# Narrowing of the third and fourth dense weight placed after the last step of attention, in a fused attention, dense layer and soft mixture of experts

## The chip, the cores and the metric

The kernel runs on one core of a Trainium2 chip. The metric is the device time of one execution in microseconds (us); the time of a kernel is the median of its runs. The engines are named as the profile names them: PE is TensorE's matmul, PEld its weight load, DVE is VectorE, ACT is ScalarE, POOL is GpSimd, SP is SyncE, whose queue issues the DMAs.

## The reference, cut

Three layers follow each other. Attention has 4 batches, 8 heads, 576 positions and head size 64, with a bias that depends on the position. A dense layer with a leaky activation (512 to 2048 to 512) works on the 2304 tokens, and a soft mixture of 8 experts comes last.

```
scores = scale * q @ k.T + bias;  attn = softmax(scores);  x = attn @ v      # x: 2304 x 512
h = x @ w_in                                       # 512 -> 2048
g = np.maximum(h, 0.0) + alpha * np.minimum(h, 0.0)
y = g @ w_out                                      # 2048 -> 512
logits = y @ phi                                   # soft mixture of experts follows
```

The dense weights are handed over as 64-bit floats, and the kernel narrows them to 32 bits itself.

## The kernel before

**Attention.** 16 pairs (four head pairs times four batches) have 9 tiles of 128 rows each, 144 tiles in all. `Attention.run` walks them two at a time in 72 steps. For one tile PE forms the scores `s` (L379), DVE adds the bias and takes the row's extreme in one custom instruction (`z`, `m`, L397), ACT takes the exponential `e` (L416), PE transposes it (`t`, L433), ACT and DVE copy the transposed halves out of PSUM (`g`, L457), and PE multiplies with `v` (`o`, L472). The scores of a tile are formed four tiles ahead. Every one of these instructions is held in the order of the program (`keep_in_program_order`), from the second pair on. PE's `o` products come in two halves per pair, 256 and 320 columns wide, each in a piece of twelve and a piece of eight records.

**The dense layer.** The 2304 tokens are six blocks (0 to 5) of 384, the 2048 hidden columns are 16 pieces `f`. For each block and piece, `up` forms `h` from `x` and the weight (L695, twelve matmuls in three terms of high and low parts), ACT takes two relus (L703, L705), DVE joins them into `g` (L706), ACT rounds `g` to its high part `gr` (L714), DVE or POOL forms the low part (L716), and `down` adds into `ys` (L728, nine matmuls). Blocks 0 and 1 run interleaved, block 1 two pieces behind.

**A dense weight's way in.** `w_load(f)` (L647, on SP's queue) brings 1 MB of 64-bit weights into one of two slots of the tile `stage`. `w_narrow(f)` makes 32-bit floats `wr` out of them with three DVE instructions (L641, L643, L644; 128 x 1024 each), and then issues `w_load(f + 2)` into the slot that it has read. `w_split` then makes the high part on ACT (L677: `w2h`, `w3h`, ...) and the low part on DVE in one piece (L679) or on POOL in four (L684). The tile `stage` lies in the space of an attention bias tile (`take_stage`, two steps before step 54), which is free when the third head pair no longer needs it. The first two weights (f = 0, 1) go another way, through the tile `early`, in twelve half pieces during attention (`half_piece`). For f = 2 and 3, `w_load` is called in step 52; their `w_narrow` is called by `prep` in `Moe.run`, behind attention, and isn't held in the order of the program. A scheduler that models the engines' times orders what isn't held; it may pull such an instruction forward in the order of its engine.

**Steps.** `extra` is a table of calls per step: `at(step, f, ...)` adds one, and `run` makes them at the step's end. Steps 46, 49, 52, 55, 64 and 69 also rescale and split columns of `x` for the dense layer (L604, L1176, L1181).

Of the kernel before, what the change touches and what calls it, by code (L numbers as in the profile page):

```python
# [67 lines left out]
NEARLY = 2  # L68
# [493 lines left out]
class Moe:  # L562
# [88 lines left out]
        pool, tag = self.homes[f] if f < len(self.homes) else (self.wring, "raw")  # L651
        return pool.tile([P, 1024], dtype, tag=tag, name=name)

    def w_narrow(self, f):

        self.raw[f] = self.raw_tile(f, f"wr{f}")
        for k in range(3):
            self.narrow(self.raw[f], self.slots[f % 2], k)
        if f + 2 < NF:
            self.w_load(f + 2)  # L660

# [464 lines left out]
def kernel(  # L1126
# [11 lines left out]
    att = Attention(tc, ident, W, xT, rs, qk, v_l)  # L1138
# [11 lines left out]
    moe = Moe(tc, ident, xT, rs, w_l, None, x0, x1)  # L1150
# [40 lines left out]
    def at(step, f, *args):  # L1191
        extra.setdefault(step, []).append(lambda: f(*args))
# [7 lines left out]
        at(step + 1, x_low, blk, c, c % 2)  # L1200
    for k in range(6 * NEARLY):
        at(HSTEPS[k], moe.half_piece, k // 3, k % 3)
    at(STAGE - 2, take_stage)
    for f in range(2):
        at(STAGE - 2, moe.w_load, NEARLY + f)
# [142 lines left out]
```

## Time and profile before

| what | value |
|---|---|
| median of 3 runs | 843.49 us |
| lowest and highest | 841.05 and 844.2 us |
| the profiled execution | 850.17 us |
| its span in the trace | 848.4 us |
| PE busy in the span | 779.9 us (92%) |
| DVE busy in the span | 550.8 us (65%) |

All stretches are given in the span's own time, counted from its start. Attention's scores start at 85.8 us, its last product ends at 341 us; the dense layer follows, and the first product of the experts starts at 791.6 us. A busy share is an average over these stages. What a moved instruction is worth is read in the stretch that it leaves and in the one that it enters.

### The profile page before, as it was taken

To read this page: it belongs to the slowest core of one execution; us is meant where nothing else is said; L and a number is where in the kernel's file an instruction comes from. 1 tells how busy PE (TensorE), PEld (TensorE's weight loads), DVE (VectorE), ACT (ScalarE), POOL (GpSimd) and SP (SyncE) were. 2 spreads that over 40 slices of the span, in tenths; PEclk is the share of its full clock that TensorE was granted. 3 is DMA by queue.
4 is the path that set the end of the run, shared out by engine and by line. 5 is a ranking of instruction groups with operands and counts; after the bars stand their busy time and mean duration, and the time that the engine had idled before them with its cause. 6 is when DMAs were issued, how large, how long until landed. Compare 5 with 4: busy or idle time off the path is not lost.

```text
span 848.4 us, 18810 instructions
## 1 busy us (share of the span) xinstructions
PE 779.9 (92%) x7444; PEld 641.5 (76%) x7444; DVE 550.8 (65%) x1058; ACT 489.6 (58%) x1066; POOL 334.6 (39%) x423
## 2 busy tenths in 40 slices
PE   6875698999998999999999999999999999998993
PEld 6875576777765777898899888888888889987341
DVE  8765477888989986899434746575656546555102
ACT  8832466787777686443445665656556556655002
POOL 6974243555464330414323352435345233242000
PEclk9989598999999899999999999999999999999897
DMA  6799994863947421365100200050010005338985
GB/s 205 180 215 199 217 215 149 215 197 117 250 121 252 146 77 48 123 221 203 45 0 1 66 10 1 2 188 10 1 29 1 1 5 187 107 110 292 412 353 224
DMA packets 59784, 114.46 MB, mean 135 GB/s; under 512 B 10672, under 2 KB 38192, under 8 KB 57904
## 3 DMA queue, kind: packets, MB, share of 16 engines
q1 hardware_dynamic: 59696, 113.26, 43.9%
q8 instruction: 58, 0.95, 0.5%
q14 instruction: 30, 0.25, 0.1%
HBM read 91.95 MB, written 21.29 MB: 133 GB/s over the span
## 4 chain that ended last, share of the span: by engine, by line
PE 62%; DMA 17%; DVE 13%; ACT 3%; issue 3%; SPq 1%; POOL 0%; DVEq 0%; ACTq 0%; POOLq 0%
PE ys L728 17%; PE h L695 17%; PE o L472 9%; PE s L379 6%; PE t L433 6%; DMA ep<-in_mw_dram 4%; PE acc L165 3%; DMA rb<-rs 3%; DMA W<-rows 3%; DMA stage<-in_w_dram 2%; DMA xT<-xo 2%; DVE wr L643 2%; DVE mask L149 2%; DVE wr L644 2%; DMA em<-in_mw_dram 1%
## 5 line engine op out<-in xcount | busy, mean ns | idle before, releaser
L706 DVE SCALAR_TENSOR_TENSOR g<-g,nal 128x384 f32<-128x384 f32 x96 | 73.2, 763 | 83.6 <-ACT g L705 83.4
L416 ACT ACTIVATE e<-z,m 128x576 f32<-128x576 f32 x144 | 110.4, 767 | 3.5 <-DVE m L397 3.2
L397 DVE CUSTOM_DVE_ANT_0 z<-s,nb 128x576 f32<-128x576 f32 x144 | 103.4, 749 | 11.5 <-PE s L379 5.6
L714 ACT ACTIVATE gr<-g 128x384 fp32r<-128x384 f32 x95 | 49.8, 524 | 98.8 <-DVE g L706 98.8
L433 PEld LDWEIGHTS t<-ident,e 64*128 64x128 f32 x1440 | 68.7, 144 | 49.0 <-ACT g L457 12.2
L457 ACT ACTIVATE g<-t 128x320 f32<-128x320 f32 x144 | 62.2, 432 | 60.6 <-PE t L433 47.4
L433 PE MATMUL t<-ident,e 64*128 64x64 f32 x1440 | 81.8, 234 | 16.3 <-ACT g L457 9.2
L472 PE MATMUL o<-g,v 128*64 128x256 f32 (+1 forms) x640 | 94.6, 418 | 0.0
L457 DVE COPY g<-t 128x320 f32<-128x320 f32 x144 | 69.5, 486 | 30.8 <-PE t L433 25.4
L165 PE MATMUL acc<-wp,mask 128*128 128x64 bf16 (+1 forms) x1680 | 60.3, 202 | 19.7 <-issue 8.5
L716 DVE TENSOR_TENSOR gr<-g,gr 128x384 fp32r<-128x384 f32 x79 | 52.8, 668 | 34.0 <-ACT gr L714 33.9
L165 PEld LDWEIGHTS <-mask 128*128 128x128 bf16 (+1 forms) x1680 | 58.0, 106 | 21.9 <-issue 12.5
L703 ACT ACTIVATE g<-h 128x384 f32<-128x384 f32 x96 | 46.6, 485 | 43.3 <-PE h L695 41.2
L379 PE MATMUL s<-kh,qh 64*128 64x288 f32 x320 | 61.0, 352 | 10.0 <-DVE rows L190 5.8
L345 POOL TENSOR_SCALAR qh<-raw 128x608 fp32r<-128x608 f32 x32 | 21.8, 698 | 114.2 <-PE s L379 109.8
L716 POOL TENSOR_TENSOR gr<-g,gr 128x384 fp32r<-128x384 f32 x16 | 20.9, 1308 | 109.6 <-ACT gr L714 106.1
L472 PEld LDWEIGHTS o<-g,v 128*64 128x64 f32 x640 | 41.2, 137 | 24.7 <-issue 0.7
L146 ACT ACTIVATE mask<-pr,wb 128x576 bf16<-128x576 f16 (+4 forms) x81 | 46.9, 669 | 22.4 <-PE acc L165 22.4
L379 PE MATMUL s<-kh,ql 64*128 64x288 f32 x320 | 53.9, 309 | 0.0
L379 PE MATMUL s<-kl,qh 64*128 64x288 f32 x320 | 53.9, 309 | 0.0
L348 POOL TENSOR_TENSOR ql<-raw,qh 128x304 fp32r<-128x304 f32 x64 | 53.1, 862 | 0.0
L705 ACT ACTIVATE g<-h 128x384 f32<-128x384 f32 x96 | 46.5, 485 | 0.0
(1008 smaller groups left out, 2058.4 us busy)
## 6 DMA issues: line engine op xcount, KB each, us to landing
ep<-in_mw_dram SPq DMA_DIRECT2D x30, 512.0 KB
raw<-in_qk_dram SPq DMA_DIRECT2D x16, 896.0 KB
stage<-in_w_dram SPq DMA_DIRECT2D x14, 1024.0 KB
nb<-W SPq DMA_DIRECT2D x12, 576.0 KB
v<-in_v_l_dram SPq DMA_DIRECT2D x16, 320.0 KB
pre<-in_mw_dram SPq DMA_DIRECT2D x10, 512.0 KB
ex<-in_mw_dram SPq DMA_DIRECT2D x9, 512.0 KB
em<-in_mw_dram SPq DMA_DIRECT2D x8, 512.0 KB
```

Source lines behind the costliest of these rows:

```text
L165: nc.tensor.matmul(dst[:, u // 8, :, :, 4 * (u % 8) : 4 * (u % 8) + 4], mask[:, (16 * k + u) % RING, cols], wp[:, part], start=part == 0, ...
L348: self.nc.gpsimd.tensor_tensor(st[x, 1][:, c], src[:, c], st[x, 0][:, c].bitcast(F32), ALU.subtract)
L379: nc.tensor.matmul(s[:, hf, :288], st["q", a][d, o : o + P], st["k", b][d, 288 * h : 288 * h + 288], start=n_ == 0, stop=n_ == len(seq) - 1,),
L397: nc.vector.tensor_tensor_reduce(out=z.rearrange("p (a b) -> p a b", a=2), in0=s[:, :, :288], in1=self.nb[st["hp"]][:, self.SLOT[t]].rearr ...
L416: self.pin(i, nc.scalar.activation(e, z, AF.Exp, bias=m, scale=-1.0, accum_out=acc))
L433: self.pin(i, nc.tensor.transpose(tp[r][:, c], e[q, k0 : k0 + P], self.ident[q, q]))
L457: self.pin(i, nc.vector.tensor_copy(dst, src) if r else nc.scalar.activation(dst, src, AF.Copy))
L472: nc.tensor.matmul(o[64 * h : 64 * h + 64, :n], st["v"][:, h, c], g[:, c, :n], start=c == 0, stop=c == 4),
L695: nc.tensor.matmul(h, w_[:, c * P : (c + 1) * P], x_[:, c], start=c == 0 and n_ == 0, stop=c == NC - 1 and n_ == 2,)
L706: nc.vector.scalar_tensor_tensor(g, neg, self.nal[:, f : f + 1], g, ALU.mult, ALU.add)
L716: eng.tensor_tensor(gl, g, gh.bitcast(F32), ALU.subtract)
L728: i = self.nc.tensor.matmul(self.ys[blk][t], g_[:, t * P : (t + 1) * P], w_[:, 512:], start=f == 0 and n_ == 0, stop=f == NF - 1 and n_ == 2,)
```

## The change

`w_narrow` gets a flag that holds its three DVE instructions in the order of the program, and the calls for f = 2 and f = 3 are entered in the table for step 72 (16 * 9 // 2), the last pass of attention's loop. `prep` then finds both weights there and no longer calls it. The two `w_load`s that `w_narrow` issues, for f = 4 and 5, move along. Nothing is computed otherwise.

```diff
-    def w_narrow(self, f):
+    def w_narrow(self, f, pin=False):
 
         self.raw[f] = self.raw_tile(f, f"wr{f}")
         for k in range(3):
-            self.narrow(self.raw[f], self.slots[f % 2], k)
+            i = self.narrow(self.raw[f], self.slots[f % 2], k)
+            if pin:
+                self.tc.keep_in_program_order(i)
         if f + 2 < NF:
             self.w_load(f + 2)
 ...
     for k in range(6 * NEARLY):
         at(HSTEPS[k], moe.half_piece, k // 3, k % 3)
+    for f in range(NEARLY, NEARLY + 2):
+        at(len(att.pairs) * 9 // 2, moe.w_narrow, f, True)
     at(STAGE - 2, take_stage)
```

In the order lists below, a name such as `g11_1_1` carries the pair (11), `z12_2` the pair and the tile, and a line from 661 on is two higher after the change than before.

On DVE, at the change from pair 11 to pair 12 (a row with - stands there only before):

```order
-L641 TENSOR_SCALAR wr2_7253<-stage_5923 128x1024
-L643 SCALAR_TENSOR_TENSOR wr2_7253<-stage_5923,wr2_7253 128x1024
 L457 COPY g11_1_1_5890<-t11_6_1_5909 128x5x64
 L493 RECIPROCAL r11_5941<-r11_5941 128x9
 L397 ISA z12_2_5959,m12_2_5960<-s12_2_5926,nb3_5498 128x576
 L397 ISA m12_2_5960 128x1
-L644 SCALAR_TENSOR_TENSOR wr2_7253<-stage_5923,wr2_7253 128x1024
-L641 TENSOR_SCALAR wr3_7322<-stage_5923 128x1024
 L397 ISA z12_3_5962,m12_3_5963<-s12_3_5933,nb3_5498 128x576
```

Four of the six narrowing instructions stand here before; the other two follow within the next ten rows. After the change the copies, `z` and `m` of attention follow each other.

On DVE, at the end of attention (`rt15` is the last copy of pair 15, `xo15_1` its last output), before:

```order
L457 COPY rt15_7164<-t15_8_1_7151 9x64
L706 SCALAR_TENSOR_TENSOR g32_7200<-g32_7200,nal_2237 128x384 x2
L480 COPY xo15_1_7184<-o15_1_7173 128x320
L641 TENSOR_SCALAR wr4_7388<-stage_5923 128x1024
L641 TENSOR_SCALAR wr5_7451<-stage_5923 128x1024
L643 SCALAR_TENSOR_TENSOR wr4_7388<-stage_5923,wr4_7388 128x1024
L643 SCALAR_TENSOR_TENSOR wr5_7451<-stage_5923,wr5_7451 128x1024
L679 TENSOR_TENSOR w3l_7328<-wr3_7322,w3h_7327 128x1024
```

and after:

```order
L643 SCALAR_TENSOR_TENSOR wr2_7173<-stage_5923,wr2_7173 128x1024
L708 SCALAR_TENSOR_TENSOR g32_7210<-g32_7210,nal_2237 128x384
L644 SCALAR_TENSOR_TENSOR wr2_7173<-stage_5923,wr2_7173 128x1024
L641 TENSOR_SCALAR wr3_7178<-stage_5923 128x1024
L643 SCALAR_TENSOR_TENSOR wr3_7178<-stage_5923,wr3_7178 128x1024
L708 SCALAR_TENSOR_TENSOR g32_7210<-g32_7210,nal_2237 128x384
L644 SCALAR_TENSOR_TENSOR wr3_7178<-stage_5923,wr3_7178 128x1024
L480 COPY xo15_1_7194<-o15_1_7183 128x320
L718 TENSOR_TENSOR gr_7211<-g32_7210,gr_7211 128x384
L641 TENSOR_SCALAR wr4_7388<-stage_5923 128x1024
L681 TENSOR_TENSOR w3l_7328<-wr3_7178,w3h_7327 128x1024
```

The narrowing of weights 2 and 3 now stands ahead of the last output copy and of the narrowing of weight 4, whose load is issued when weight 2 is done.

On PE, behind attention's last product (`h2` is block 1 with weight 0, `h3` block 0 with weight 2, `h4` block 1 with weight 1), before:

```order
L695 MATMUL h2_7295<-x1_5575,w0l_6338 128x384
L728 MATMUL ys0_0_7283<-w0h_6337,gr_7201 128x512
L728 MATMUL ys0_0_7283<-w0l_6338,gr_7201 128x512
...
L728 MATMUL ys0_2_7285<-w0h_6337,gr_7201 128x512
L695 MATMUL h3_7331<-x0_2240,w2h_7258 128x384 x2
L695 MATMUL h3_7331<-x0_2240,w2l_7259 128x384
```

and after:

```order
L697 MATMUL h2_7300<-x1_5575,w0l_6338 128x384
L697 MATMUL h3_7331<-x0_2240,w2h_7263 128x384 x2
L697 MATMUL h4_7361<-x1_5575,w1h_6544 128x384 x2
L697 MATMUL h4_7361<-x1_5575,w1l_6545 128x384
...
L697 MATMUL h4_7361<-x1_5575,w1h_6544 128x384
L697 MATMUL h3_7331<-x0_2240,w2l_7264 128x384
```

PE comes to weight 2 right behind `h2` now; before, the nine products into `ys0` stood between. The products into `ys0` with weights 0 and 1 come after `h3` and `h4` now.

## Rows read from the trace of the kernel before

**Rows 1.** The page's part 1: busy us (share of the span) and instructions.

```profile
PE 779.9 (92%) x7444; PEld 641.5 (76%) x7444; DVE 550.8 (65%) x1058; ACT 489.6 (58%) x1066; POOL 334.6 (39%) x423
```

**Rows 2.** DVE in order of time, 270 to 282 us: start, us, instruction, [idle before].

```profile
270.26 0.87 DVE L641 TENSOR_SCALAR wr<-stage 128x1024 uint32<-128x1024 uint32 x1 [1.09 <-DMA stage<-in_w_dram]
271.17 1.23 DVE L643 SCALAR_TENSOR_TENSOR wr<-stage,wr 128x1024 uint32<-128x1024 uint32 x1
...
273.45 1.22 DVE L644 SCALAR_TENSOR_TENSOR wr<-stage,wr 128x1024 uint32<-128x1024 uint32 x1
274.59 0.69 DVE L641 TENSOR_SCALAR wr<-stage 128x1024 uint32<-128x1024 uint32 x1
...
277.26 1.20 DVE L643 SCALAR_TENSOR_TENSOR wr<-stage,wr 128x1024 uint32<-128x1024 uint32 x1
...
280.15 1.20 DVE L644 SCALAR_TENSOR_TENSOR wr<-stage,wr 128x1024 uint32<-128x1024 uint32 x1
```

**Rows 3.** Waits of PE, 266 to 290 us: us in total, times, longest.

```profile
PE s L379 <- DVE m L397: 2.2, 3, 1.8
PE t L433 <- DVE g L457: 2.0, 1, 2.0
PE t L433 <- ACT g L457: 0.7, 2, 0.3
```

**Rows 4.** Busy time by stretch: stretch, us, PE, PEld, DVE, ACT, POOL, granted clock, DMA.

```profile
272.00:276.00 4.00, 1.24 (x18) 0.83 (x18) 4.00 (x10) 1.29 (x4) 0.00 (x0) 0.99 0.94 334
276.00:280.00 4.00, 3.41 (x32) 3.00 (x34) 4.00 (x10) 2.31 (x6) 0.00 (x0) 0.50 0.75 274
280.00:284.00 4.00, 4.00 (x38) 2.92 (x34) 3.98 (x9) 1.26 (x4) 0.00 (x0) 0.66 0.40 123
266.68:289.30 22.62, 17.77 (x214) 13.32 (x210) 20.25 (x43) 13.07 (x37) 8.06 (x11) 0.85 0.71 259
301.70:316.90 15.20, 14.39 (x210) 10.91 (x210) 12.74 (x36) 12.34 (x35) 3.52 (x5) 1.00 0.24 75
360.00:380.00 20.00, 20.00 (x103) 18.11 (x102) 19.29 (x23) 7.28 (x15) 2.75 (x2) 1.00 0.61 214
```

**Rows 5.** DVE in order of time, from attention's last copy on.

```profile
338.35 0.20 DVE L457 COPY rt<-t 9x64 f32<-9x64 f32 x1
342.03 1.28 DVE L641 TENSOR_SCALAR wr<-stage 128x1024 uint32<-128x1024 uint32 x2
343.23 3.44 DVE L643 SCALAR_TENSOR_TENSOR wr<-stage,wr 128x1024 uint32<-128x1024 uint32 x2
355.05 0.85 DVE L641 TENSOR_SCALAR wr<-stage 128x1024 uint32<-128x1024 uint32 x1 [1.41 <-DMA stage<-in_w_dram]
...
402.80 1.75 DVE L644 SCALAR_TENSOR_TENSOR wr<-stage,wr 128x1024 uint32<-128x1024 uint32 x1
```

**Rows 6.** ACT, POOL and the issue of weight 6's load, in order of time.

```profile
340.12 0.47 ACT L705 ACTIVATE g<-h 128x384 f32<-128x384 f32 x1
341.49 1.06 ACT L677 ACTIVATE w2h<-wr 128x1024 fp32r<-128x1024 f32 x1 [0.90 <-PE o L472]
342.63 6.33 POOL L684 TENSOR_TENSOR w2l<-wr,w2h 128x256 fp32r<-128x256 f32 x4 [1.34 <-ACT w2h L677]
350.06 43.82 SPq L647 DMA_DIRECT2D stage<-in_w_dram  x10
```

**Rows 7.** PE in order of time, from attention's last product on.

```profile
341.38 0.62 PE L695 MATMUL h<-x,w0h 128*128 128x384 f32 x2
343.58 0.40 PE L728 MATMUL ys<-w0h,gr 128*128 128x512 f32 x1
354.01 0.51 PE L695 MATMUL h<-x,w3h 128*128 128x384 f32 x2
363.07 0.51 PE L695 MATMUL h<-x,w4h 128*128 128x384 f32 x2
423.08 0.51 PE L695 MATMUL h<-x,w11h 128*128 128x384 f32 x2
```

## The prediction

> **What bounds the kernel now.** The page's part 1 comes first: PE is busy for 779.9 of 848.4 us [rows 1], so a gain has to be time in which PE waits or runs slowly. In the stretch that the change empties, around the change from pair 11 to pair 12, PE isn't the bound. DVE's rows in order of time show six narrowing instructions between attention's copies [rows 2]: the first waited 1.09 us for its DMA, which it does at the head of DVE's queue, so that the copies and `z` behind it stood too. The list of PE's waits shows who paid: PE lost 2.2 us to `m` and 2.0 us to copies on DVE, and 0.7 us to ACT, which is fed by the same chain [rows 3]. Then read the table of stretches [rows 4]: in 272 to 276 us DVE is busy for all of the 4.00 us and PE for 1.24; PE's granted clock is still 0.99 there, and in the next two stretches 0.50 (the lower level, 1.2 GHz) and 0.66. Behind the end of attention it is otherwise: in 360 to 380 us PE is busy for 20.00 of 20.00 us at full clock, with DVE at 19.29 right behind it [rows 4].
>
> **What is taken out of attention.** I measure the loss between equal points, PE's first piece of a 256-wide product. The stretch with the narrowing is 22.62 us long, the one two pairs later, with as many tiles, 15.20; PE has 214 and 210 records in them, DVE 43 and 36, and six of the 43 are the narrowing [rows 4]. The difference is 22.62 - 15.20 = 7.4 us. Two other sums agree. On PE, the waits are 2.2 + 2.0 + 0.7 = 4.9 us [rows 3]; the clock costs 4.0 x (1 - 0.50) + 4.0 x (1 - 0.66) = 3.4 us [rows 4]; of the 8.3, the later stretch has 15.20 - 14.39 = 0.8 us without PE too [rows 4], which leaves 7.5. On DVE, the six take 0.87 + 1.23 + 1.22 + 0.69 + 1.20 + 1.20 = 6.4 us, and with the wait of 1.09 that is 7.5 [rows 2]. Without them DVE has 20.25 - 6.4 = 13.9 us of work in some 15.2, so it fits, closely. **I take -7.4**; the bounds are -4.1 (only the waits go, 4.9 - 0.8, and the clock falls all the same) and -8.3 (nothing of the later stretch's idle time comes back here). The loads of weights 4 and 5 go out of this stretch as well; nobody here waits for them, and the DMA share of 0.94 and 0.75 in it [rows 4] can only fall.
>
> **What is put into the end of attention.** The loads of weights 2 and 3 have long landed there, so no wait for them goes along. DVE is free at 338.35 + 0.20 = 338.55 us [rows 5]. Its new order is L641 (0.7), the join of `h0` (0.6), L643 (1.2), the join of `h1` (0.6; ACT's relu ends at 340.6 [rows 6], in time), L644 (1.2): weight 2 is narrow at 342.8. The bound is the two L643 that ran beside POOL and took 3.44 / 2 = 1.72 each [rows 5] instead of 1.2; POOL makes low parts here too, so 343.8 is the other end. ACT's high part takes 1.06 [rows 6]: ready at 343.9, or 344.9. PE is done with `h2` when it was before, at 343.58 [rows 7], and now asks for weight 2 at once: it waits 0.3 to 1.3 us. Two matmuls later it asks for `h4`, whose PSUM buffer was `h2`'s; ACT's two relus on `h2` (0.47 each [rows 6]) stand behind the high part, which costs PE another 0.5. **So PE waits 0.8 to 1.8 us, and I take 0.8**, since the isolated durations of [rows 2] are nearer to what stands there than the four long POOL pieces beside which 1.72 was measured.
>
> Behind that I find no wait. POOL's first piece of `w2l` takes 6.33 / 4 = 1.58 [rows 6] and is there at 345.5 (346.5), while PE has the rest of `h4` before it. Weight 3 is narrow 0.7 + 1.2 + 0.6 + 1.2 = 3.7 us (with long instructions 4.8) after weight 2, at 346.5 to 348.6. Its low part stands behind the first instruction of weight 4, and so behind a DMA: that load is issued when weight 2 is done, and weight 6's took from 350.06 [rows 6] to 355.05 [rows 5], 5.0 us. So DVE waits to 347.8 (348.8), takes 0.85 [rows 5] and makes `w3l` in 1.2 to 1.7: ready by 351.4. PE came to weight 3 at 354.01 [rows 7], and now does `h4` and all of `ys0` first. Weight 4 is narrow some 4 us after weight 3's low part; PE asks for it at 363.07 [rows 7]. Later the moved 6.4 us of DVE work eat into a lead: DVE finished its last weight, the sixteenth, at 402.80 + 1.75 [rows 5], and PE asked for the twelfth at 423.08 [rows 7]. The last output copy of attention comes some 5 us later on DVE, and its store on SP stands behind the load of weight 5; its reader stands behind ten more loads, which took 43.82 us [rows 6]. These edits I cost at nothing; if the lead were gone, all 6.4 would be PE's.
>
> **A rule that speaks against it.** Measured: a long narrowing instruction beside POOL's pieces took 0.5 us more (1.72 against 1.20 to 1.23), and POOL was at 0.00 busy where it took the short time [rows 2, 4, 5]. The Trainium skill says (SBUF — State Buffer, "Who interferes with whom") that a VectorE instruction with two SBUF inputs and a GpSimd instruction that reads SBUF exclude each other: whichever starts first holds the shared ports for its whole length and the other fully blocks. By that, the sum here would have a whole POOL piece in place of 0.5 for each collision; the trace's 0.5 doesn't bear out so much.
>
> **The sum.** -7.4 + 0.8 = -6.6 us. The profiled execution, 850.17 us with a span of 848.4, would be 843.6; it lies 6.7 us over the median of the runs, so I carry the difference to the median: 843.49 - 6.6 = 836.9 us. The stages behind keep their length, since their loads start when PE's and DVE's work frees buffers: a shift, no new wait.
>
> **The rivals.**
> - *The clock falls anyway.* DVE is left with 13.9 of some 15.2 us, and a small pause could still bring the lower level. Against it: the later stretch ran at 1.00 with its 0.8 us of idle PE [rows 4]. Gain 4.1 - 0.8 = 3.3: 840.2 us.
> - *Whole POOL pieces.* Each of weight 2's two long instructions stands a piece of 1.58 us [rows 6], 3.2 more for PE: 843.49 - 7.4 + 0.8 + 3.2 = 840.1 us. This is the page's rule as a mechanism of this kernel.
> - *DVE becomes the bound.* With 19.29 of 20 us busy [rows 4], the 6.4 moved microseconds could land on PE in full: 843.49 - 7.4 + 6.4 = 842.5 us. For it: DVE's share. Against it: the lead of the narrowing over PE [rows 5, 7], and that DVE had waits for loads there (1.41 [rows 5]).
> - *Slower: the load of weight 4.* Before, it lay ready; now it is issued at 343, and DVE stands at its head with everything for PE behind it. If `h3`'s join and the split of weight 3 fall behind it for its full 5.0 us and DVE is the bound too, it is 6.4 + 5.0 + 0.8 - 7.4 = +4.8: 848.3 us. It decides where weight 3's low part comes later than PE's 354.01; my working has 351.4.
> - *The change doesn't do what it says*: the order lists show that it does.
>
> **How the numbers follow.** Forecast 0.71 (its own range 835 to 839), clock 0.07, POOL 0.03, DVE bound 0.11, slower 0.08. A measurement of this kernel tells about 0.5%, 4.2 us, from no change. Faster by more is the forecast, 0.71; within are clock, POOL and DVE bound, 0.21; slower 0.08. The range goes from -8.3 without a cost, and 1 us for the medians, 834.0, to the DVE-bound case, 842.6; above it lie the slower case and a part of that one, some 0.15, below it 0.04.
>
> **What would show it.** No L641 to L644 between 266 and 290 us, and the same stretch near 15.2 us with the granted clock at 1.00 (wrong: it stays over 17, or a clock of 0.50 stands in it). Behind attention's last product, PE's waits for ACT's `w2h` and `h2` sum to 0.8 to 1.8 us (wrong: over 3). DVE's first wait for `stage` is at weight 4, and `w3l` is done before PE comes to it. The stretch from attention's last product to the experts' first keeps its length within 2 us.

## The result, and the profile after

The changed kernel takes 836.75 us (median of 4 runs, 835.96 to 837.26); the kernel before, beside it, took 842.32 (4 runs, 841.05 to 844.2). The ratio is 0.9913, with an interval of 0.9884 to 0.9941. Two further comparisons below, with more runs of the kernel before, gave 0.9910 [0.9895, 0.9925] and 0.9916 [0.9886, 0.9947]. The three differences are 5.6, 7.3 and 7.1 us. The forecast was 836.9 us.

The page's part 1 of the kernel after, which answers to [rows 1]: PE is busy for 7.6 us less, and DVE has as much to do as it had. Not all of the 7.6 is the change's: the matmuls of L165, which it doesn't move, are busy for 57.2 us here and for 60.3 in the trace of before.

```profile
PE 772.3 (92%) x7444; PEld 636.0 (76%) x7444; DVE 551.8 (66%) x1058; ACT 489.4 (59%) x1066; POOL 332.9 (40%) x423
```

**The stretch that was emptied.** PE's rows in order of time (start, us), at the two ends of the stretch from pair 11 to pair 12; then PE's waits in 263 to 290 us (us in total, times, longest), which answer to [rows 3]; then busy time by stretch (stretch, us, PE, PEld, DVE, ACT, POOL, granted clock, DMA), which answers to [rows 4].

```profile
263.82 1.52 PE L472 MATMUL o<-g,v 128*64 128x256 f32 x12
...
279.43 1.52 PE L472 MATMUL o<-g,v 128*64 128x256 f32 x12
```

```profile
PE t L433 <- ACT g L457: 0.6, 2, 0.3
```

```profile
263.82:279.43 15.61, 14.98 (x212) 11.09 (x208) 14.33 (x37) 12.68 (x37) 8.01 (x11) 1.00 0.63 239
272.00:276.00 4.00, 4.00 (x60) 2.88 (x57) 3.39 (x9) 2.65 (x8) 0.68 (x2) 1.00 0.21 78
...
360.00:380.00 20.00, 20.00 (x101) 17.77 (x100) 19.93 (x24) 7.59 (x15) 2.74 (x2) 1.00 0.61 211
```

The stretch is 15.6 us long instead of 22.6. The waits for `m` and for DVE's copies are gone, and the clock is 1.00 throughout, where [rows 4] had 0.50 and 0.66. In 360 to 380 us, which PE still fills, DVE has gone from 19.29 to 19.93 of 20 us. The same work lies 9.8 us earlier now; in 350.2 to 370.2 us DVE has 19.69.

**The end of attention.** DVE in order of time, which answers to [rows 5]; behind it ACT, POOL and the issue of the loads of weights 4 and 5 [rows 6], and PE [rows 7]. In brackets is the idle time before a row and what ended it.

```profile
328.64 0.67 DVE L641 TENSOR_SCALAR wr<-stage 128x1024 uint32<-128x1024 uint32 x1
...
329.77 1.21 DVE L643 SCALAR_TENSOR_TENSOR wr<-stage,wr 128x1024 uint32<-128x1024 uint32 x1
...
332.18 1.21 DVE L644 SCALAR_TENSOR_TENSOR wr<-stage,wr 128x1024 uint32<-128x1024 uint32 x1
333.31 1.50 DVE L641 TENSOR_SCALAR wr<-stage 128x1024 uint32<-128x1024 uint32 x1
334.84 1.64 DVE L643 SCALAR_TENSOR_TENSOR wr<-stage,wr 128x1024 uint32<-128x1024 uint32 x1
...
337.42 1.76 DVE L644 SCALAR_TENSOR_TENSOR wr<-stage,wr 128x1024 uint32<-128x1024 uint32 x1
...
340.12 0.68 DVE L641 TENSOR_SCALAR wr<-stage 128x1024 uint32<-128x1024 uint32 x1
340.73 1.21 DVE L681 TENSOR_TENSOR w3l<-wr,w3h 128x1024 fp32r<-128x1024 f32 x1
```

```profile
332.89 1.36 POOL L718 TENSOR_TENSOR gr<-g,gr 128x384 fp32r<-128x384 f32 x1 [1.06 <-ACT gr L716]
334.62 5.16 POOL L686 TENSOR_TENSOR w2l<-wr,w2h 128x256 fp32r<-128x256 f32 x4 [0.36 <-ACT w2h L679]
333.49 1.06 ACT L679 ACTIVATE w2h<-wr 128x1024 fp32r<-128x1024 f32 x1 [0.67 <-DVE wr L644]
334.82 0.48 ACT L707 ACTIVATE g<-h 128x384 f32<-128x384 f32 x1
333.42 6.15 SPq L647 DMA_DIRECT2D stage<-in_w_dram  x2
```

```profile
334.60 0.61 PE L697 MATMUL h<-x,w2h 128*128 128x384 f32 x2 [0.69 <-ACT w2h L679]
335.36 0.61 PE L697 MATMUL h<-x,w1h 128*128 128x384 f32 x2
...
345.58 0.51 PE L697 MATMUL h<-x,w3h 128*128 128x384 f32 x2
```

PE waits 0.69 us for `w2h`. Weight 3's low part is ready at 341.94 (340.73 + 1.21), and PE asks for weight 3 at 345.58. The six narrowing instructions, 6.4 us in attention, take 8.0 here.

**Where the time went.** One trace's span is a few microseconds from the next one's, also in parts that the change doesn't touch: the stretch starts at 266.68 us in the trace of before, at 263.21 in a second one. So the account goes between marks on PE, each the start of a row: the start of the stretch, its end, the next such mark, attention's last product, the first matmul with weight 8 (`w8h`), and the experts' first product with `ep`. In us:

| kernel | the stretch | next | to the last product | to weight 8 | to the experts | sum |
|---|---|---|---|---|---|---|
| before | 22.6 | 12.4 | 36.2 | 58.7 | 395.0 | 524.9 |
| before, second trace | 22.3 | 12.4 | 36.3 | 58.6 | 394.5 | 524.0 |
| after | 15.6 | 12.4 | 36.2 | 59.6 | 394.1 | 517.9 |
| after, second trace | 15.6 | 12.4 | 36.2 | 59.4 | 393.4 | 517.1 |
| after, third trace | 15.6 | 12.4 | 36.2 | 59.5 | 393.8 | 517.5 |

By the means the stretch gives 6.8 us, the passage into the dense layer costs 0.9, and the rest of the dense layer is 1.0 shorter: 6.9 in all. The 13.0 us between the two first spans (848.4 and 835.4) holds trace-to-trace variation besides.

### The profile page after: what moved, and what is told of

Its sections match the earlier page's. It is cut to its first block, busy times and chain, and to the rows that moved or that the text cites. A ratio compares the mean times of both kernels' runs of the same rounds, so it can differ in the third digit from the quotient of the medians.

```text
span 835.4 us, 18819 instructions
## 1 busy us (share of the span) xinstructions
PE 772.3 (92%) x7444; PEld 636.0 (76%) x7444; DVE 551.8 (66%) x1058; ACT 489.4 (59%) x1066; POOL 332.9 (40%) x423
## 4 chain that ended last, share of the span: by engine, by line
PE 43%; DMA 4%; DVE 3%; ACT 1%; issue 1%; SPq 0%; DVEq 0%; ACTq 0%
PE ys L730 18%; PE h L697 18%; DMA ep<-in_mw_dram 2%; PE hps L1084 2%; DMA rb<-rs 1%; PE lp L789 1%; PE sp L849 0%; PE sp L848 0%; DVE vv L604 0%; DVE g L708 0%; PE tl L836 0%; DVE x L610 0%; DVE gr L718 0%; DMA vv<-xT 0%; PE tc L898 0%
## 5 line engine op out<-in xcount | busy, mean ns | idle before, releaser
L165 PE MATMUL acc<-wp,mask 128*128 128x64 bf16 (+1 forms) x1680 | 57.2, 198 | 22.4 <-issue 14.8
L165 PEld LDWEIGHTS <-mask 128*128 128x128 bf16 (+1 forms) x1680 | 54.9, 103 | 24.5 <-issue 17.4
L379 PE MATMUL s<-kh,qh 64*128 64x288 f32 x320 | 60.3, 346 | 7.3 <-DVE rows L190 5.4
L146 ACT ACTIVATE mask<-pr,wb 128x576 bf16<-128x576 f16 (+4 forms) x81 | 47.1, 666 | 22.3 <-PE acc L165 22.2
```

Of the source, the lines that this page charges most:

```text
L165: nc.tensor.matmul(dst[:, u // 8, :, :, 4 * (u % 8) : 4 * (u % 8) + 4], mask[:, (16 * k + u) % RING, cols], wp[:, part], start=part == 0, ...
L379: nc.tensor.matmul(s[:, hf, :288], st["q", a][d, o : o + P], st["k", b][d, 288 * h : 288 * h + 288], start=n_ == 0, stop=n_ == len(seq) - 1,),
```

## The experiments

**Both kernels again.** No edit; the traces of the table.

> The kernel before, once more, for a second trace of it. My theory (what the change saves is the stretch around the change from pair 11 to 12, by DVE's six narrowing instructions there): the time is that of the kernel before, 842.3 us within 0.3%; the stretch between PE's 256-wide products is 22.6 us again, with a granted clock near 0.5 in it, and what the first trace has longer ahead of 255 us and behind 790 us than the trace after differs from trace to trace. The rival (the 13 us between the two spans are all the change's): those two parts are as long as in the first trace.

Measured: 843.62 us (12 runs) against 844.24 of the same kernel (17 runs), ratio 0.9993 [0.9979, 1.0007].

> The changed kernel once more, beside the others on one chip. My theory: 836.7 us, 5.6 us less than before, the stretch 15.2 to 15.6 us long at full clock, PE's wait for the high part of weight 2 behind attention 0.7 us. The rival (a part of the difference of the first runs was the chip's): under 3 us less than before.

Measured: 836.95 us (836.78 to 837.38, 5 runs), 7.3 less than 844.24. The account between marks holds in a second pair of traces. Their spans, 841.6 and 834.9 us, differ by 6.7, so the rest of the first pair's 13.0 is not the change's.

**Only weight 3 moved.** Weight 2 goes back to where the scheduler puts it.

```diff
-    for f in range(NEARLY, NEARLY + 2):
-        at(len(att.pairs) * 9 // 2, moe.w_narrow, f, True)
+    at(len(att.pairs) * 9 // 2, moe.w_narrow, NEARLY + 1, True)
```

> Half of the change: weight 3 is narrowed in step 72, weight 2 stays free, and the scheduler leaves it in attention where it was. My theory (DVE's work and the wait for the load, each by its length): 1.1 us of wait and 3.3 us of work stay in attention, 3.1 us go out, and behind attention PE has no wait for weight 2: 842.3 - 3.1 = 839.2 us. The rival (the first wait and the pause that it makes cost nearly all, and the clock falls as before): 841.5 us or more. The rival that DVE copes with one weight: 837 us.

Measured: 843.46 us (12 runs), ratio to before 0.9989 [0.9970, 1.0008]. Half the work is gone from the stretch, and next to nothing is gained: the stretch is still 21.5 us. My theory that each instruction costs by its length (839.2) falls; the rival in which the first wait and the pause cost nearly all (841.5 or more) fits. DVE in order of time, PE's waits in 255 to 325, and three stretches of this kernel:

```profile
266.32 1.23 DVE L604 TENSOR_TENSOR vv<-vv 128x384 f32<-128x384 f32 x1
268.42 1.09 DVE L641 TENSOR_SCALAR wr<-stage 128x1024 uint32<-128x1024 uint32 x1 [0.88 <-DMA stage<-in_w_dram]
269.55 1.22 DVE L643 SCALAR_TENSOR_TENSOR wr<-stage,wr 128x1024 uint32<-128x1024 uint32 x1
270.69 0.48 DVE L457 COPY g<-t 128x320 f32<-128x320 f32 x1
```

```profile
PE t L433 <- DVE g L457: 2.0, 1, 2.0
...
PE s L379 <- DVE m L397: 1.3, 2, 1.1
```

```profile
268.00:272.00 4.00, 1.81 (x28) 0.97 (x24) 3.54 (x7) 2.45 (x9) 0.96 (x2) 1.00 1.01 408
272.00:276.00 4.00, 2.52 (x25) 2.08 (x27) 4.00 (x10) 1.71 (x6) 0.00 (x0) 0.65 0.82 252
276.00:280.00 4.00, 4.00 (x39) 3.62 (x41) 2.85 (x9) 2.36 (x7) 0.00 (x0) 0.50 0.50 198
```

What counts is how long DVE stays away from the copies that PE needs: from 266.32 to 270.69 us, 4.4 us in a row, made of a rescaling (L604), the wait for the DMA and two narrowing instructions. PE runs out of work, is busy for 1.81 of 4.00 us, and in the next two stretches the granted clock is 0.65 and 0.50 (the lower level, 1.2 GHz). In the kernel before, the rest of the narrowing stood beside a PE already slowed by this first part. That the first part starts it is seen; that the second weight was cheap because PE was slow is my reading of it.

**The block without a DMA wait, whole and halved.** Both weights, then weight 2 alone, as one uninterrupted block in step 58, where the loads have landed.

```diff
-        at(len(att.pairs) * 9 // 2, moe.w_narrow, f, True)
+        at(58, moe.w_narrow, f, True)
```

> Both weights are narrowed in attention as before, but held in step 58, where their loads have landed: six instructions in one block, no wait for a DMA. My theory (DVE's work ahead of attention's chain costs): PE pauses for some 4 us or more and the clock falls, so only the wait of 1.1 us is saved, and the attention stretch that holds the block is 6 us longer than without: 841 us. The rival (the wait for the load at the head of DVE's queue is what starts the pause): 837 to 838 us, with the clock at 1.00.

```diff
-        at(len(att.pairs) * 9 // 2, moe.w_narrow, f, True)
+        at((58, len(att.pairs) * 9 // 2)[f - NEARLY], moe.w_narrow, f, True)
```

> Half of the block: only weight 2 is narrowed, as one block, in step 58, weight 3 stays behind the last step as in the changed kernel. With both, the block held DVE from 282.88 to 289.11 us, 6.2 us, PE's wait for a copy behind it was 2.9 us, and the interval grew by 5.6 us. Theory, the lead: PE had 6.2 - 2.9 = 3.3 us of work left when DVE turned away, so a block of 3.1 us is just hidden: PE's wait for DVE is under 0.5 us, the granted clock stays 1.00, and the interval is 12.4 to 13.0 us. Rival A, every microsecond of the block costs alike: half of 5.6, 15.2 us. Rival B, the first weight in the way costs most, as in the run with the third weight left in attention: 16 to 17.5 us with the clock under 0.9 in the stretch behind. The whole kernel by the lead: within 0.8 us of the changed kernel, since the transition is 0.4 to 0.8 shorter without weight 2; by A +2.4, by B +3.5.

Measured: whole, 843.61 us (12 runs), ratio to before 0.9988 [0.9974, 1.0001], and the interval behind the stretch is 18.0 us instead of 12.4; halved, 837.07 us (835.21 to 838.21, 4 runs), ratio 0.9893 [0.9864, 0.9922], and the interval is 13.3. The whole block is above both what I expected (841) and the rival's 837 to 838: that it doesn't wait for a DMA saves nothing that can be told. From the whole block: DVE's first and last narrowing and its next copy, PE's wait for DVE in 255 to 325, and three stretches.

```profile
282.88 0.67 DVE L641 TENSOR_SCALAR wr<-stage 128x1024 uint32<-128x1024 uint32 x1
...
287.97 1.23 DVE L644 SCALAR_TENSOR_TENSOR wr<-stage,wr 128x1024 uint32<-128x1024 uint32 x1
289.11 0.48 DVE L457 COPY g<-t 128x320 f32<-128x320 f32 x1
```

```profile
PE t L433 <- DVE g L457: 2.9, 1, 2.9
```

```profile
286.00:290.00 4.00, 1.06 (x14) 0.49 (x10) 3.93 (x6) 0.00 (x0) 0.00 (x0) 1.00 0.75 257
290.00:294.00 4.00, 3.83 (x33) 2.65 (x31) 3.50 (x11) 2.39 (x6) 2.06 (x4) 0.62 0.86 309
294.00:298.00 4.00, 4.00 (x56) 2.60 (x54) 2.81 (x7) 2.74 (x8) 4.00 (x6) 0.95 0.47 127
```

And from the halved block, the same:

```profile
283.31 0.67 DVE L641 TENSOR_SCALAR wr<-stage 128x1024 uint32<-128x1024 uint32 x1
...
286.42 0.48 DVE L457 COPY g<-t 128x320 f32<-128x320 f32 x1
```

```profile
286.00:290.00 4.00, 3.81 (x46) 2.39 (x44) 4.00 (x11) 2.21 (x7) 1.06 (x2) 1.00 0.68 201
```

The halved block keeps DVE away for 3.1 us: no wait of PE for DVE is in the list, the clock stays at 1.00, and the cost is 0.9 us, a little above the 0 to 0.6 that I expected. The second half costs 4.7 more, though it is equally long. The 5.6 us of the whole block nearly add up: a wait of 2.9, a clock loss of 4 x (1 - 0.62) + 4 x (1 - 0.95) = 1.7, and the 0.9 of the half block. So the price is not by the microsecond; in this place PE had 6.2 - 2.9 = 3.3 us of work ahead, and what goes beyond that is paid in full and again in clock. "Each microsecond alike" (15.2 us) and "the first weight costs most" (16 to 17.5) both fall: it was not the first weight but its place behind L604 and a DMA wait.

**In steps 70 and 71.** The same two calls, one step apart, shortly before the end of attention.

```diff
-        at(len(att.pairs) * 9 // 2, moe.w_narrow, f, True)
+        at(70 + f - NEARLY, moe.w_narrow, f, True)
```

> Weight 2 is narrowed in step 70 and weight 3 in step 71 in place of step 72. My theory: DVE has idle time in the last steps, since the row extremes of the last tiles are long done, so PE's wait of 0.7 us for weight 2 goes and nothing else comes: 836.0 us, 0.7 less than the changed kernel. The rival (the copies of the last tiles stand behind the narrowing on DVE and PE waits for them): 837 to 838 us, with waits of PE for DVE's copies in the last 10 us of attention.

Measured: 839.42 us (838.18 to 840.95), ratio to before 0.9938 [0.9922, 0.9954], 2.5 more than the changed kernel. My theory was wrong and the rival right in kind, though the time is above its 837 to 838. PE's waits for DVE in 300 to 420:

```profile
PE t L433 <- DVE g L457: 1.3, 1, 1.3
...
PE o L472 <- DVE g L457: 0.5, 1, 0.5
```

The wait for `w2h` is gone, but attention's copies now stand behind narrowing again. The two times away from the copies are 4.5 and 3.5 us in that trace, and less the waits they leave 3.2 and 3.0 us: PE's lead, near the 3.3 of step 58.

**One instruction per step.** Six steps with one narrowing instruction each; the second kernel spreads weight 2 alone and leaves weight 3 behind the last step. The changed kernel ran beside the latter.

```diff
+    def n_piece(self, f, k):
+        if k == 0:
+            self.raw[f] = self.raw_tile(f, f"wr{f}")
+        self.tc.keep_in_program_order(self.narrow(self.raw[f], self.slots[f % 2], k))
+        if k == 2 and f + 2 < NF:
+            self.w_load(f + 2)
 ...
-    for f in range(NEARLY, NEARLY + 2):
-        at(len(att.pairs) * 9 // 2, moe.w_narrow, f, True)
+    for k, step in enumerate((57, 59, 61, 66, 67, 68)):
+        at(step, moe.n_piece, NEARLY + k // 3, k % 3)
```

> The six narrowing instructions are held one by one in steps 57, 59, 61 (weight 2), 66, 67 and 68 (weight 3), inside attention, long after their loads have landed. My theory (it is DVE's work that costs, as far as DVE has no idle time beside attention): two stretches of attention of 15.2 us have some 2.5 us of idle DVE each, so one or two of the 6.4 us show and PE's wait for weight 2 of 0.7 goes: 837 to 838.5 us. The rival that only the wait for the load at the head of DVE's queue cost: all hidden, 836.0 us. The rival that every narrowing instruction in attention delays PE by its length: 836.7 - 0.7 + 6.4 = 842.4 us.

```diff
-    for k, step in enumerate((57, 59, 61, 66, 67, 68)):
-        at(step, moe.n_piece, NEARLY + k // 3, k % 3)
+    for k, step in enumerate((57, 59, 61)):
+        at(step, moe.n_piece, NEARLY, k)
+    at(len(att.pairs) * 9 // 2, moe.w_narrow, NEARLY + 1, True)
```

> Weight 2's three narrowing instructions go one by one into steps 57, 59 and 61 of attention; weight 3 stays behind the last step, as in the changed kernel. My theory: one narrowing instruction in a step that has no wait for a DMA in front of it is carried by DVE's slack, as the run with all six pieces spread showed for its first three (12.68 against 12.37 in the interval of steps 57 to 61, +0.3), and the transition gets rid of 3.1 us of DVE work, PE's wait for w2h (0.7) with it, so it takes 58.3 to 58.7 instead of 59.4: 0.4 to 0.8 less than the changed kernel, 836.2 where that has 836.9. Rival A, order of the dense part: any change of what is there at attention's end makes the scheduler lay out the later part differently, and the dense part from weight 8 to the experts is 395.8 instead of 393.4 to 394.5, as with all six spread: 838 to 839. Rival B, DVE has no slack in attention: +3.1 us, 840.

> The changed kernel again, on the same chip as its neighbour, as the mark that the neighbour is compared with: 836.5 to 837.4, 59.4 us from attention's last product to weight 8, 0.7 us of PE's wait for w2h, and a stretch of 15.6 at pair 12.

Measured: all six spread, 839.35 us (838.52 to 839.87), ratio to before 0.9935 [0.9920, 0.9950], above what I expected. Weight 2 alone, 838.88 (837.98 to 840.25, 6 runs), ratio 0.9927 [0.9901, 0.9953], against 837.81 (836.03 to 840.96, 6 runs) of the changed kernel, so no gain. Between the marks, the two are 517.8 and 517.5 us: the passage to weight 8 is 0.4 shorter (59.1 us; I expected 58.3 to 58.7), and attention is 0.6 longer (12.7 instead of 12.4 in the interval of steps 57 to 61, and 0.1 in each of the two behind it). What is spared behind attention is paid inside it.

All six spread cost 2.4 us more than the changed kernel, 519.9 between the marks. 0.3 of it is in the interval of steps 57 to 61, and 1.2 is one wait of PE for a copy. PE's row, then SP and DVE of that kernel:

```profile
328.74 3.27 PE L472 MATMUL o<-g,v 128*64 128x320 f32 x20 [1.21 <-DVE g L457]
```

```profile
315.65 0.36 SPq L647 DMA_DIRECT2D stage<-in_w_dram  x1
316.11 1.09 SPq L601 DMA_DIRECT2D rb<-rs  x2
322.67 0.56 DVE L604 TENSOR_TENSOR vv<-vv,rb 128x384 f32<-128x384 f32 x1 [4.03 <-DMA rb<-rs]
...
327.63 0.56 DVE L604 TENSOR_TENSOR vv<-vv,rb 128x384 f32<-128x384 f32 x1 [1.86 <-DMA vv<-xT]
328.11 0.88 DVE L457 COPY g<-t 128x320 f32<-128x320 f32 x2
```

The copy that PE waits for stands behind a rescaling (L604) that waited 1.86 us for `vv`; in the changed kernel that wait is 0.65. Five us earlier the first L604 waited 4.03 us for `rb`, against 2.13 in the changed kernel and 2.19 in the one with weight 2 alone. The load of weight 5, which follows its slot's narrowing, is issued right ahead of that load of `rb`, at 315.65; with weight 2 alone it is issued at 333.23. That the late `rb` makes the next loads and so `vv` late too is my reading of these rows; no run moved the load alone. The 4.03 us themselves cost PE nothing: DVE is away from the copies from 318.11 to 323.14, 5.0 us, and PE has products of the dense layer (`h` with weights 0 and 1) to do and doesn't wait.

Another 2.0 lies between weight 8 and the experts (395.8 us), against which the passage is 1.3 shorter. In 420 to 780 us this kernel has two waits that the changed one has not:

```profile
PE ys L738 <- ACT gr L724: 1.6, 2, 1.0
...
PE h L705 <- DVE w19l L689: 0.4, 1, 0.4
```

**Weight 3 narrowed twice.** Its three instructions run two times in step 72; the second time they write the same values again, in 0.68 + 1.21 + 1.22 = 3.1 us more of DVE's work.

```diff
-        for k in range(3):
+        for k in (0, 1, 2) * (1 + (pin and f == 3)):
```

> The changed kernel with the narrowing of weight 3 done twice in step 72, 3.1 to 4.8 us more of DVE's work behind attention, same values. My theory (behind attention the narrowing leads PE, and only weight 2 is late): the low part of weight 3 comes within 1 us of when PE asks for it, 836.7 to 837.7 us. The rival (DVE bounds the stretch behind attention, so the 6.4 us that moved there cost PE what they last): 3.4 us or more over the changed kernel, 840 us.

Measured: 843.46 us (841.53 to 847.11, 12 runs), ratio to before 0.9987 [0.9970, 1.0004]: 6.5 more than the changed kernel. My expectation, that the lead hides it, is off by far, and the rival's 840 is too low as well. PE's waits of this kernel in 328 to 394 us, and the load that came late:

```profile
PE ys L730 <- ACT gr L716: 1.6, 2, 1.4
PE h L697 <- DVE w3l L681: 1.5, 1, 1.5
PE ys L730 <- DVE gr L718: 1.4, 1, 1.4
...
```

```profile
350.73 0.70 DVE L641 TENSOR_SCALAR wr<-stage 128x1024 uint32<-128x1024 uint32 x1 [0.93 <-DMA stage<-in_w_dram]
```

From attention's last product to weight 8 it is 66.4 us, 6.8 more than in the changed kernel, at a clock of 1.00 (in 345 to 350, 350 to 355 and 360 to 365 us PE is busy for 3.33, 3.62 and 3.64 of 5 us, with 1.00 granted each time). The waits sum to 5.8 us, against 0.7 there. 3.1 us on DVE thus cost twice that on PE: the load of weight 5 is issued later too, DVE waits 0.93 for it, and the low parts of `gr` that PE waits for stand behind narrowing. The split between these I didn't measure.

## Why the prediction was right

**The stretch, -7.4.** Measured -6.7 to -7.0. The stretch is 15.6 us and not 15.2: the pattern stretch two pairs later was not quite the same, since DVE has 14.33 us of work here and PE 14.98, against 12.74 and 14.39 in [rows 4]. The clock stays at 1.00, so the rival in which it falls all the same is out. The sums by PE's waits and clock and by DVE's work were both right in size, but the second was right by luck: 7.5 us of DVE's time cost 7.5 because a 4.4 us absence from the copies started the pause and the clock loss, and not because each of the six instructions cost its length. The run that moved weight 3 alone shows the difference: by length it would have kept about half of the gain, and it kept none that can be told.

**The passage into the dense layer, +0.8.** Measured +0.7 to +1.0 between marks. The wait for `w2h` was put at 0.3 to 1.3 and is 0.69. For `h4` behind ACT's relus I had 0.5: the second relu ends at 334.82 + 0.48 = 335.30 and PE's `h4` starts at 335.36, right behind the two matmuls on `w2h`. That chain exists, but the gap that it leaves on PE is only 0.15 us (334.60 + 0.61 to 335.36), so this term was sized too high and the other too low for the middle of its bounds. That the sum came out has a part of luck besides. The passage of before held a wait of 0.44 us for `gr` (350.95) that is gone now, so PE's time without work there rises by only 0.4 us (from 0.44 to 0.83). The other 0.5 is busy time as the profile models it, 58.74 us instead of 58.22 with as many matmuls, and was in no term. The kernel that moves only weight 3 has it too: its passage takes 59.15 us with PE busy for 58.66, and no wait for `w2h`. What makes it stays open.

PE before, in the passage:

```profile
350.95 0.95 PE L728 MATMUL ys<-w1h,gr 128*128 128x512 f32 x3 [0.44 <-POOL gr L716]
```

**No wait behind that.** Weight 3's low part was ready at 341.94, 3.6 us before PE asked; the forecast, counted from attention's last product of before (9.8 us later there), was 341.6. But DVE's first wait for `stage` was said to be at weight 4, and that is wrong: the load issued at 333.42 has landed when DVE comes to it at 340.12, behind the output copy and a low part of `gr` that I had not put there, though the order list shows both. DVE also came later because weight 3 was narrow 5.8 us behind weight 2 (339.18 and 333.39), where I had 3.7 to 4.8. The first such wait is 0.21 us, at weight 7. So the rival with the load of weight 4 didn't come. In sum over the kernel DVE's waits for `stage` went from 3.1 to 0.2 us (busy groups by line and form, first of before, then of after; the last two numbers are the idle time and its releaser):

```profile
L641 DVE TENSOR_SCALAR wr<-stage 128x1024 uint32<-128x1024 uint32 x14 | 11.3, 814 | 3.2 <-DMA stage<-in_w_dram 3.1
```

```profile
L641 DVE TENSOR_SCALAR wr<-stage 128x1024 uint32<-128x1024 uint32 x14 | 11.7, 838 | 0.2 <-DMA stage<-in_w_dram 0.2
```

About 1.1 of that was the wait in attention, the rest was time behind attention that the moved work could fill. The rival in which DVE becomes the bound was nearer than its 0.11 says: 3.1 us more there cost 6.8.

**The rule on shared ports.** Weight 2's two long instructions took 1.21 us each, not the 1.72 of the bound; both were running already when POOL's next piece began (330.48 and 332.89). Others were stretched: L641 1.50 instead of 0.67 us, L643 and L644 1.64 and 1.76 instead of 1.21, beside POOL's `gr` and `w2l` pieces (5.16 / 4 = 1.29 each). The rival charged whole pieces of 1.58 for each of weight 2's instructions, and that didn't happen. Yet the dismissal was too quick. L641 started at 333.31 while POOL's `gr` ran from 332.89 to 334.25, which leaves 0.94 of that, and it was 0.83 longer; this is near what the rule of the Trainium skill (SBUF — State Buffer, "Who interferes with whom") gives if only the rest of the piece already running blocks. For an instruction with one SBUF input, as L641 is, that section says so only of a mode that uses both ports; its 0.67 us against the 1.21 of the two-input ones would fit such a mode, but no row names it. The 0.43 of L643 is far less than the rest of its piece. POOL's spans are rough, so these runs don't decide it.

**The stages behind, unchanged.** Between weight 8 and the experts it is 1.0 us shorter, which I hadn't in the sum. PE's waits for `gr` and `w19l` there come to 3.0 and 2.7 us in the two traces of before and to 1.8 to 2.0 in the three of the changed kernel, which doesn't wait for `w19l` (0.5 and 0.6 before). With all six spread they are 3.0 and with the whole block 2.9, so the two other kernels that narrow both weights well ahead of attention's end are like before. The order of the later dense pieces differs between the kernels, and which change of it does this I haven't tested.

In all, -6.8 + 0.9 - 1.0 = -6.9 us where the forecast had -7.4 + 0.8 = -6.6. The mechanism is the forecast's, but that the sum is this near is in part luck: 0.6 less came from the stretch, and 1.0 that was in no term made up for it. So is the match of 836.9 with 836.75. The forecast counted from a median of 843.49, and the kernel before took 842.32 beside the changed one and 844.24 and 844.88 later, with 836.95 and 837.81 for the changed one.

Two ends of the range are off their own terms: 843.49 - 8.3 - 1 is 834.2 and not 834.0, and the DVE-bound case is 842.5 and not 842.6. Neither matters for the outcome.

## What to carry to other kernels

On an engine that works its queue in order, price a foreign block by how long the next consumer goes without its input, less the consumer's lead at that place, and add what the pause costs in clock; a block within the lead is nearly free, one well beyond it is not. The lead is no constant: it was 2.4 to 3.3 us in most places here, 1.4 in one, and 5 or more where PE had products of the dense layer to fill in. A DMA wait in that queue counts towards the absence. Before moving such work to where an engine has little idle time, add some more of it there on the chip: the passage here took six instructions of 6.4 us for 0.9, and the next three, of 3.1 us, cost 6.8.

## What was not expected of the hardware

- A DVE absence of 3.1 us cost PE 0.9 us, one of 6.2 us cost 5.6. Absences of 3.5, 4.5 and 6.2 us left PE waits of 0.5, 1.3 and 2.9 us, each 3.0 to 3.3 less; the 4.4 us with the rescaling in it left 2.0. But 5.0 us (the first L604 with all six spread) left none, and 2.6 us a little later (from 325.51 to 328.11) left 1.2.
- Behind a pause in which PE was busy for 1.06 of 4.00 us the granted clock was 0.62 over the next 4 us and 0.95 over the 4 after that; behind 1.81 of 4.00 it was 0.65 and then 0.50. In the passage of the kernel that narrows weight 3 twice, PE at 3.33 of 5.00 kept 1.00.
- With a 1 MB load issued 0.5 us ahead of a small one, DVE waited 4.0 us for the small one instead of 2.1. No run moved the load alone.
